# A fixed order for every engine in a window-attention and SoLU kernel: four engines' instruction order moved from the tile scheduler to a list made in the kernel

## The chip, the cores and the metric

The kernel runs on one NeuronCore of a Trainium2 chip. Five engines work beside each other, each on its own queue of instructions in order: TensorE (PE) multiplies matrices, VectorE (DVE) and ScalarE (ACT) work elementwise, GpSimd (POOL) does elementwise work too but only on SBUF here, and SyncE (SP) issues the DMA transfers. The metric is the device time of one execution in microseconds (us), the median of several.

## The reference

Attention over a sliding window of 64 positions, for 8 batches of 576 positions and 8 heads of 64, and then a layer of 512 to 1024 to 512 with a softmax-weighted activation and a normalization:

```python
def _attn_ref(q, k, v):
    scores = scale * np.matmul(q, k.transpose(0, 1, 3, 2))
    mask = (rel >= 0) & (rel < window)
    scores = np.where(mask, scores, -1000000000.0)
    scores = scores - np.max(scores, axis=-1, keepdims=True)
    attn = np.exp(scores)
    attn = attn / (np.sum(attn, axis=-1, keepdims=True) + 1e-09)
    return np.matmul(attn, v)

def _moe_ref(x, w_in, w_out, g_ln):
    h = x @ w_in
    e = np.exp(h - np.max(h, axis=-1, keepdims=True))
    solu = h * (e / (np.sum(e, axis=-1, keepdims=True) + 1e-09))
    mu = np.mean(solu, axis=-1, keepdims=True)
    var = np.mean((solu - mu) ** 2, axis=-1, keepdims=True)
    ln = (solu - mu) / np.sqrt(var + 1e-06) * g_ln
    return ln @ w_out
```

The weights come as float64 and q, k, v as float32.

## The kernel before

The 4608 positions are cut into 36 tiles of 128. What happens to tile t:

- `load` brings q, k and two halves of v by DMA.
- `attn_scores`: PE makes pS (8 heads, one buffer); DVE adds the mask and takes the maxima, eight instructions (L184); ACT takes eight exps (L188); DVE makes the reciprocals (L192, L193); POOL scales by them, eight instructions (L195). The result is sS.
- `attn_transpose`: PE transposes sS into pA, two times four heads; ACT and DVE copy one half each to PT (L206).
- `attn_values`: PE makes pX; ACT rounds it to xH (L224), and DVE makes the rest, xL (L225).
- `moe_in`: 24 matmuls of 128x512 (L237) in two halves of 12 make ph, the first layer in three products (high times high, high times low, low times high). The texts call this ph(t). There is one ph buffer.
- `moe_norm` reads ph: DVE's maximum (L248), ACT's exp (L249), DVE's product (L250); then small DVE steps, ACT's square (L255), more small steps (L256, L257, L259), POOL's power (L258) and the normalization in two halves (L262).
- `moe_transpose` (PE into pT, ACT's yH, DVE's yL) and `moe_out` (24 matmuls, L284, the second layer; the texts call them po(t)), then ACT's copy ot and a store.

The weights are float64 in HBM, and before use each is taken apart into a high and a low part on the chip. This goes in 16 blocks of 128x512, eight for each layer. A block is: a load of 0.5 MB (wi_raw or wo_raw, four buffers), ACT's Abs (L112), four DVE instructions (L113 to L116), for the second layer a product with g on POOL (L118), ACT's cast to the high part (L119) and POOL's difference, the low part (L120). Three work buffers (wi_t, wo_t) hold blocks in progress.

The loop runs 39 iterations. Iteration t does the first half of ph(t), the transposes of tile t+1, the second half of ph(t), the norm of t, then the transposes of the second layer for tile t-3, the values of t+1, the scores of t+3, and po(t-3). Ahead of the loop stand the loads of tiles 0 to 3, the eight blocks of the first layer, and scores, transposes and values of the first tiles. The second layer's eight blocks are written in iterations 0 and 1; they are first needed in iteration 3, at po(0).

PE keeps the order in which the kernel is written (`manual_schedule` names PE alone). The order of the other engines, and of SP's transfers, is chosen by the tile framework's scheduler, which runs a timeline of its own and takes an instruction earlier where it stands in `tc.high_priority(offset=URGENT)`: the copies out of PSUM, and L248 to L250.

Of the kernel before, what the change touches and what calls it, by code (L numbers as in the profile page):

```python
# [32 lines left out]
def tile_window_attention_solu_moe(
# [67 lines left out]
    live = {}  # L101

    def weight_block(src, wH, wL, g, name):

# [7 lines left out]
        nc.scalar.activation(tf, hi.bitcast(F32), AF.Abs)  # L112
        nc.vector.tensor_scalar(tf, tf, EXP_LO, EXP_HI, ALU.max, ALU.min)  # L113
        nc.vector.tensor_scalar(t, t, 0x07FFFFFF, 3, ALU.bitwise_and, ALU.logical_shift_left)  # L114
        nc.vector.scalar_tensor_tensor(t, hi, -0x40000000, t, ALU.bitwise_and, ALU.bitwise_or)  # L115
        nc.vector.scalar_tensor_tensor(t, lo, 29, t, ALU.logical_shift_right, ALU.bitwise_or)  # L116
# [2 lines left out]
        nc.scalar.copy(wH, tf)  # L119
        nc.gpsimd.tensor_sub(wL, tf, wH.bitcast(F32))  # L120

    def prep_in(c, h):
        hs = slice(h * 512, (h + 1) * 512)
        weight_block(
            w_in[c * P:(c + 1) * P, 2 * h * 512:2 * (h + 1) * 512],
            w_inH[:, c, hs], w_inL[:, c, hs], None, f"wi_{c}_{h}")

    def prep_out(f):
        weight_block(
            w_out[f * P:(f + 1) * P, :], w_outH[:, f], w_outL[:, f], g_sb[:, f:f + 1], f"wo_{f}")  # L130
# [4 lines left out]

    def load(t):
        first = first_of(t)
        o = t * P
# [20 lines left out]
        live["qk", t] = q, k
        live["v", t] = vv  # L160

    def attn_scores(t):
# [4 lines left out]
        for p in range(NPAIR):
            for half in range(2):
                for r in range(2):
                    rs = slice(r * D, (r + 1) * D)  # L170
# [5 lines left out]
                    nc.tensor.matmul(  # L176
                        pS[half * WIN:(half + 1) * WIN, r, p],
                        q[rs, p, half * WIN:(half + 1) * WIN], keys, start=True, stop=True)
        sS = sb.tile([P, H, P], F32, tag="sS", name=f"sS_{t}", bufs=3)
        nmx = st.tile([P, H], F32, tag="nmx", name=f"nmx_{t}")  # L180
        sm = st.tile([P, H], F32, tag="sm", name=f"sm_{t}")
        for h in range(H):

            nc.vector.tensor_tensor_reduce(  # L184
                sS[:, h], pS[:, h % 2, h // 2], masks[first], scale=-SCALE, scalar=BIG,
                op0=ALU.add, op1=ALU.min, accum_out=nmx[:, h:h + 1])
        for h in range(H):
            nc.scalar.activation(  # L188
                sS[:, h], sS[:, h], AF.Exp, bias=nmx[:, h:h + 1], scale=-1.0,
                accum_out=sm[:, h:h + 1])  # L190
        rec = st.tile([P, H], F32, tag="rec", name=f"rec_{t}")
        nc.vector.tensor_scalar_add(rec, sm, 1e-9)  # L192
        nc.vector.reciprocal(rec, rec)  # L193
        for h in range(H):
            nc.gpsimd.tensor_scalar(sS[:, h], sS[:, h], rec[:, h:h + 1], 0.0, ALU.mult, ALU.add)  # L195
# [161 lines left out]
```

## Time and profile before

| what | value |
|---|---|
| median of 3 runs | 615.12 us (615.04 to 616.85) |
| the profiled execution itself | 617.23 us |
| its span, first to last instruction | 615.4 us |
| mean granted TensorE clock | 0.972 |
| PE matmuls busy | 568.9 us, 92% |
| DVE, ACT, POOL busy | 316.3, 310.7, 217.7 us |

The span is what the profile's views cover; the time of an execution is 1.8 us more. A profile is of one execution. Every view names instructions by engine, by line of the kernel (L237 is line 237), and by tiles, output ahead of input, with buffer numbers left out. A wait is put down to what ended it. PE's busy time includes matmuls that only run slowly because the granted clock is low, so clock and busy time are read together.

### The profile page before, as it was taken

The numbers are of one execution on the slowest core, as the hardware profiler recorded it, in microseconds if no ns is written. First come the engines' busy times: TensorE is split into PE (matmuls) and PEld (weight loads), VectorE is DVE, ScalarE is ACT, GpSimd is POOL, SyncE is SP. The second block draws the span as 40 slices with busy tenths as digits, with TensorE's granted clock in tenths as the row PEclk, the third lists the DMA queues.
The fourth block names the chain that finished last, engine by engine and source line by source line (L and its number), as shares of the span: only waits on it lengthen the run. The fifth ranks groups of instructions, "written<-read, shape, count | busy, mean of one in ns | idle before, by whom it ended". The sixth has DMA issues, their size and how long they took to land.

```text
span 615.4 us, 12587 instructions
## 1 busy us (share of the span) xinstructions
PE 568.9 (92%) x4608; PEld 461.7 (75%) x4608; DVE 316.3 (51%) x1180; ACT 310.7 (50%) x933; POOL 217.7 (35%) x438
## 2 busy tenths in 40 slices
PE   1566589999999999999999999999999999999997
PEld 1334468888888888888888888888888888888775
DVE  2788955444444444444444455555454444443430
ACT  3555566555555555555555555555555555553331
POOL 2686864333333333333333333333333333331110
PEclk9966889999999999999999999999999999999999
DMA  8974422333333323333333333323333321000000
GB/s 280 322 227 158 134 78 79 96 99 98 98 98 98 96 94 96 95 95 95 95 96 95 95 95 96 95 95 95 95 95 95 95 95 53 18 18 18 18 35 34
DMA packets 56205, 60.97 MB, mean 99 GB/s; under 512 B 3408, under 2 KB 40272, under 8 KB 56144
## 3 DMA queue, kind: packets, MB, share of 16 engines
q1 hardware_dynamic: 56144, 60.18, 30.9%
q8 instruction: 36, 0.59, 0.4%
q14 instruction: 25, 0.20, 0.1%
HBM read 50.73 MB, written 9.44 MB: 98 GB/s over the span
## 4 chain that ended last, share of the span: by engine, by line
PE 86%; DVE 5%; POOL 3%; ACT 2%; DMA 1%; issue 1%; SPq 1%; POOLq 0%; ACTq 0%
PE po L284 34%; PE ph L237 31%; PE pX L218 6%; PE pS L176 5%; PE pA L204 5%; PE pT L273 5%; POOL sS L195 2%; DMA wi_raw<-w_in 1%; ACT sS L188 1%; DVE wo_t L113 1%; DVE wo_t L115 1%; POOL w_inL L120 1%; DVE e L250 1%; DVE wi_t L116 1%; DVE wo_t L114 0%
## 5 line engine op out<-in xcount | busy, mean ns | idle before, releaser
L237 PE MATMUL ph<-w_inH,xH 128*128 128x512 f32 x288 | 120.5, 419 | 14.1 <-DVE mst L250 6.1
L258 POOL TENSOR_TENSOR mst<-mst,neghalf 128x1 f32<-128x1 f32 x36 | 19.9, 554 | 317.2 <-DVE mst L257 317.2
L237 PE MATMUL ph<-w_inL,xH 128*128 128x512 f32 x288 | 117.6, 408 | 6.1 <-POOL w_inL L120 6.1
L284 PE MATMUL po<-w_outH,yH 128*128 128x512 f32 x288 | 117.7, 409 | 1.2 <-ACT yH L276 1.2
L237 PE MATMUL ph<-w_inH,xL 128*128 128x512 f32 x288 | 117.5, 408 | 0.5 <-DVE mst L252 0.5
L195 POOL TENSOR_SCALAR sS<-sS,rec 128x128 f32<-128x128 f32 x288 | 109.4, 401 | 18.0 <-ACT ot L287 10.0
L284 PE MATMUL po<-w_outH,yL 128*128 128x512 f32 x288 | 114.3, 397 | 0.0
L284 PE MATMUL po<-w_outL,yH 128*128 128x512 f32 x288 | 113.9, 395 | 0.0
L188 ACT ACTIVATE sS<-sS,nmx 128x128 f32<-128x128 f32 x288 | 111.2, 388 | 5.0 <-DVE nmx L184 5.0
L276 ACT CAST yH<-pT 128x512 fp32r<-128x512 f32 x72 | 38.7, 589 | 106.2 <-PE pT L273 106.2
L248 DVE TENSOR_REDUCE mst<-ph 128x1 f32<-128x1024 f32 x36 | 44.1, 1224 | 74.3 <-PE ph L237 74.3
L237 PEld LDWEIGHTS ph<-w_inH,xH 128*128 128x128 f32 x288 | 55.9, 194 | 27.1 <-DVE mst L250 6.4
L206 DVE COPY PT<-pA 128x512 f32<-128x512 f32 x36 | 24.9, 691 | 97.9 <-PE pA L204 97.9
L237 PEld LDWEIGHTS ph<-w_inL,xH 128*128 128x128 f32 x288 | 56.1, 195 | 19.9 <-POOL w_inL L120 8.3
L255 ACT ACTIVATE sq<-e,mst 128x1024 bf16<-128x1024 f32 x36 | 41.4, 1149 | 53.5 <-DVE mst L254 53.0
L284 PEld LDWEIGHTS po<-w_outH,yH 128*128 128x128 f32 x288 | 54.1, 188 | 18.5 <-ACT e L249 4.8
L237 PEld LDWEIGHTS ph<-w_inH,xL 128*128 128x128 f32 x288 | 56.1, 195 | 15.0 <-DVE mst L252 1.2
L284 PEld LDWEIGHTS po<-w_outH,yL 128*128 128x128 f32 x288 | 54.1, 188 | 14.6 <-DVE yL L277 1.7
L284 PEld LDWEIGHTS po<-w_outL,yH 128*128 128x128 f32 x288 | 54.2, 188 | 11.5
L262 POOL TENSOR_SCALAR e<-e,mst 128x512 f32<-128x512 f32 x72 | 55.8, 782 | 15.6 <-DVE mst L259 13.6
L206 ACT COPY PT<-pA 128x512 f32<-128x512 f32 x36 | 21.1, 586 | 78.8 <-PE pA L204 78.7
L188 ACT ACTIVATION_READ_ACCUMULATOR sS<-sS,nmx 128x1 f32 x288 | 53.8, 187 | 0.0
(59 smaller groups left out, 752.2 us busy)
## 6 DMA issues: line engine op xcount, KB each, us to landing
v<-vS SPq DMA_DIRECT2D x64, 256.0 KB, 2.9
k<-kT SPq DMA_DIRECT2D x35, 384.0 KB, 4.9
q<-qT SPq DMA_DIRECT2D x36, 256.0 KB, 4.1
y<-ot SPq DMA_DIRECT2D x36, 256.0 KB, 2.0
wi_raw<-w_in SPq DMA_DIRECT2D x8, 512.0 KB, 7.1
wo_raw<-w_out SPq DMA_DIRECT2D x8, 512.0 KB, 3.3
v<-vS SPq DMA_DIRECT2D x16, 128.0 KB, 2.9
k<-kT SPq DMA_DIRECT2D x1, 256.0 KB, 3.6
```

The costliest lines, as they stand in the source:

```text
L176: nc.tensor.matmul(pS[half * WIN:(half + 1) * WIN, r, p], q[rs, p, half * WIN:(half + 1) * WIN], keys, start=True, stop=True)
L188: nc.scalar.activation(sS[:, h], sS[:, h], AF.Exp, bias=nmx[:, h:h + 1], scale=-1.0, accum_out=sm[:, h:h + 1])
L195: nc.gpsimd.tensor_scalar(sS[:, h], sS[:, h], rec[:, h:h + 1], 0.0, ALU.mult, ALU.add)
L204: nc.tensor.transpose(pA[:, i], sS[:, 4 * x + i], ident)
L206: (nc.vector.tensor_copy if x else nc.scalar.copy)(PT[:, 4 * x:4 * x + 4], pA)
L218: nc.tensor.matmul(pX[r * D:(r + 1) * D, p, ks], vv[half][:, h * D:(h + 1) * D], PT[:, h, ks], start=True, stop=True)
L237: nc.tensor.matmul(live["h", t][:, hs], lhs[:, c], rhs[:, c, hs], start=(c == k == 0), stop=(c == NC - 1 and k == 2))
L248: nc.vector.tensor_reduce(nmax, ph, axis=AX.X, op=ALU.max, negate=True)
L255: nc.scalar.activation(sq, e, AF.Square, bias=nmean, scale=1.0, accum_out=ss)
L262: nc.gpsimd.tensor_scalar(e[:, hs], e[:, hs], nmean, kk, ALU.add, ALU.mult)
L276: nc.scalar.copy(yH[:, hs], pT)
L284: nc.tensor.matmul(po, lhs[:, f], rhs[:, f], start=(f == k == 0), stop=(f == NF - 1 and k == 2))
```

## The change

The kernel no longer leaves the order of DVE, ACT, POOL and SP to the framework. Each operation is first recorded, with its engine, a cost in ns, what it reads and writes, and a function that emits it. A ring says how many buffers a tile name has. `Plan.edges` makes dependencies from reads, writes and rings, and chains PE's operations in the order in which they are written. `Plan.order` gives each operation a due time (working back from a PE that never waits), then runs the list in time: whenever an engine is free, it takes of the operations that are ready the one that is due first. The instructions are then emitted in that order, and `manual_schedule` names all five engines. The high priorities are gone. The rings of nmx, sm and rec are 4 deep where they had 6 buffers; the others keep their depth. A score, a set of transposes and a set of values are each one operation of PE.

```diff
+RINGS = {
+    "raw": 4, "wt": 3, "q": 3, "k": 3, "v0": 4, "v1": 4, "sS": 3, "PT": 2, "xH": 2, "xL": 2,
+    "e": BEHIND + 1, "sq": 1, "yH": 1, "yL": 1, "ot": 2, "nmx": 4, "sm": 4, "rec": 4, "mst": 6,
+    "pS": 1, "pH": 1, "t": 2, "pX": 1, "pO": 1,
+}
+class Plan:
+    LATENCY = 150
...
+    def op(self, engine, cost, emit, reads, writes, lat=0):
+        self.ops.append((engine, cost, emit, reads, writes, lat + self.LATENCY))
+    def dma(self, size, emit, reads, writes):
+        self.op("SP", max(350, size // 250), emit, reads, writes, 2000)
...
+    def order(self):
...
+        clock, due = 0, [1e9] * n
+        for i, o in enumerate(self.ops):
+            if o[0] == "PE":
+                due[i] = clock
+                clock += o[1]
+        for j in reversed(topo):
+            for i, whole in after[j]:
+                lat = self.ops[j][5] if self.ops[i][0] != self.ops[j][0] else 0
+                due[j] = min(due[j], due[i] - (self.ops[j][1] + lat if whole else 0))
...
+        while any(waiting.values()):
+            begin, e = min(
+                (max(free[e], min(ready[i] for i in w)), e) for e, w in waiting.items() if w)
+            i = min((i for i in waiting[e] if ready[i] <= begin), key=lambda i: (due[i], i))
+            waiting[e].remove(i)
+            out.append(i)
+            end = begin + self.ops[i][1]
+            free[e] = end
...
-        nc.scalar.activation(tf, hi.bitcast(F32), AF.Abs)
-        nc.vector.tensor_scalar(tf, tf, EXP_LO, EXP_HI, ALU.max, ALU.min)
+        plan.op("ACT", 600, lambda: nc.scalar.activation(tf(), hi().bitcast(F32), AF.Abs), [R], [W])
+        plan.op("DVE", 420, lambda: nc.vector.tensor_scalar(
+            tf(), tf(), EXP_LO, EXP_HI, ALU.max, ALU.min), [W], [W])
...
-        with tc.high_priority(offset=URGENT):
-            nc.vector.tensor_reduce(nmax, ph, axis=AX.X, op=ALU.max, negate=True)
+        plan.op("DVE", 1150, lambda: nc.vector.tensor_reduce(
+            nmax(), PH(t), axis=AX.X, op=ALU.max, negate=True), [("pH", t)], [key(0)])
...
-    with tc.manual_schedule(engines={mybir.EngineType.PE}):
...
+    order = plan.order()
+    with tc.manual_schedule(engines={
+            mybir.EngineType.PE, mybir.EngineType.DVE, mybir.EngineType.Activation,
+            mybir.EngineType.Pool, mybir.EngineType.SP}):
+        for emit in order:
+            emit()
```

In what follows a row is an instruction as it stands on its engine: line, operation, output from input. The changed kernel's names are raw and wt for a weight block's load and work buffer (0 to 7 first layer, 8 to 15 second), t for the transposes' PSUM buffer, pH and pO for ph and po. Its lines: L257 to L263 are L113 to L116 of before, L266 is L118, L269 is L120, L353 is L184, L371 is L195, L392 is L206, L418 is L225, L449 and L454 are L248 and L250, L463 is L256.

SP at the program's start. Before:

```order
L142 DMA q_0_112<-qT 128x4x128
L146 DMA k_0_113<-kT 128x4x128
L155 DMA v0_0_116<-vS 64x512 x2
L157 DMA v1_0_119<-vS 128x512
L108 DMA wi_0_0_raw_121<-w_in 128x1024
L108 DMA wi_1_0_raw_131<-w_in 128x1024
L142 DMA q_1_188<-qT 128x4x128
```

Now:

```order
L255 DMA raw_0_112<-w_in 128x1024
L255 DMA raw_1_114<-w_in 128x1024
L255 DMA raw_2_116<-w_in 128x1024
L255 DMA raw_3_123<-w_in 128x1024
L303 DMA k_0_133<-kT 128x4x128
L300 DMA q_0_141<-qT 128x4x128
L255 DMA raw_4_148<-w_in 128x1024
```

Four weight loads have moved ahead of tile 0's q and k, and tile 0's v stands behind the fifth and sixth.

POOL from its first weight block on. Before:

```order
L120 TENSOR_TENSOR w_inL_104<-wi_0_0_t_123,w_inH_103 128x512
L195 TENSOR_SCALAR sS_0_158<-sS_0_158,rec_0_177 128x128 x8
L120 TENSOR_TENSOR w_inL_104<-wi_1_0_t_133,w_inH_103 128x512
L120 TENSOR_TENSOR w_inL_104<-wi_2_0_t_198,w_inH_103 128x512
L120 TENSOR_TENSOR w_inL_104<-wi_3_0_t_208,w_inH_103 128x512
L195 TENSOR_SCALAR sS_1_246<-sS_1_246,rec_1_265 128x128 x8
L120 TENSOR_TENSOR w_inL_104<-wi_0_1_t_307,w_inH_103 128x512
```

Now:

```order
L269 TENSOR_TENSOR w_inL_104<-wt_0_118,w_inH_103 128x512
L269 TENSOR_TENSOR w_inL_104<-wt_1_125,w_inH_103 128x512
L269 TENSOR_TENSOR w_inL_104<-wt_2_135,w_inH_103 128x512
L269 TENSOR_TENSOR w_inL_104<-wt_3_145,w_inH_103 128x512
L269 TENSOR_TENSOR w_inL_104<-wt_4_188,w_inH_103 128x512
L371 TENSOR_SCALAR sS_0_176<-sS_0_176,rec_0_211 128x128 x8
L269 TENSOR_TENSOR w_inL_104<-wt_5_213,w_inH_103 128x512
L269 TENSOR_TENSOR w_inL_104<-wt_6_242,w_inH_103 128x512
L371 TENSOR_SCALAR sS_1_271<-sS_1_271,rec_1_353 128x128 x8
```

Five first-layer blocks stand ahead of tile 0's scaling, where one stood; DVE's order at the start moved in the same way.

DVE around the first read of ph, tile 0's. Before:

```order
L116 SCALAR_TENSOR_TENSOR wo_1_t_414<-wo_1_raw_412,wo_1_t_414 128x512
L114 TENSOR_SCALAR wo_2_t_425<-wo_2_t_425 128x512
L248 TENSOR_REDUCE mst_0_492<-ph_0_454 128x1
L115 SCALAR_TENSOR_TENSOR wo_2_t_425<-wo_2_raw_423,wo_2_t_425 128x512
L113 TENSOR_SCALAR wo_3_t_436<-wo_3_t_436 128x512
L116 SCALAR_TENSOR_TENSOR wo_2_t_425<-wo_2_raw_423,wo_2_t_425 128x512
L114 TENSOR_SCALAR wo_3_t_436<-wo_3_t_436 128x512
L250 ISA e_0_493,mst_0_492<-ph_0_454,e_0_493 128x1024
```

Now:

```order
L392 COPY PT_1_401<-t_5_407 128x512
L366 TENSOR_SCALAR rec_2_422<-sm_2_377 128x8
L369 RECIPROCAL rec_2_422<-rec_2_422 128x8
L449 TENSOR_REDUCE mst_0_456<-pH_0_342 128x1
L418 TENSOR_TENSOR xL_1_484<-pX_1_438,xH_1_478 128x512
L353 ISA sS_3_486,nmx_3_487<-pS_3_460,maskNone_96 128x128
```

The second layer's blocks no longer stand around tile 0's two reads; between them are now xL and four of tile 3's scores (one is shown).

More of the change, by code (lines that the diff above doesn't have):

```diff
@@ L122, in prep_in, with T @@
[L122 to L130, printed above, removed]
+    plan = Plan(RINGS)
+    def T(tag, n, shape, dtype=F32, pool=None):
+        if (tag, n) not in plan.tiles:
+            plan.tiles[tag, n] = (pool or sb).tile(
+                shape, dtype, tag=tag, name=f"{tag}_{n}", bufs=RINGS[tag])
+        return plan.tiles[tag, n]
@@ new lines, in prep, with Q @@
+    def prep(i):
+        if i < 2 * NC:
+            h, c = divmod(i, NC)
+            hs = slice(h * 512, (h + 1) * 512)
+            weight_block(
+                i, w_in[c * P:(c + 1) * P, 2 * h * 512:2 * (h + 1) * 512],
+                w_inH[:, c, hs], w_inL[:, c, hs], None, ("in", c, h))
+        else:
+            f = i - 2 * NC
+            weight_block(
+                i, w_out[f * P:(f + 1) * P, :], w_outH[:, f], w_outL[:, f], g_sb[:, f:f + 1],
+                ("out", f))
+    def Q(t):
+        return T("q", t, [P, NPAIR, P])
@@ L136, in load, with K, V @@
+    def K(t):
+        return T("k", t, [P, NPAIR, P + WIN])
+    def V(t, half):
+        return T(f"v{half}", t, [P, DM])
     def load(t):
@@ new lines, in softmax @@
+        plan.op("DVE", 130, lambda: nc.vector.tensor_scalar_add(
+            rec(), T("sm", t, [P, H], pool=st), 1e-9),
+            [("sm", t, h) for h in range(H)], [("rec", t)])
+        plan.op("DVE", 130, lambda: nc.vector.reciprocal(rec(), rec()), [], [("rec", t)])
+        for h in range(H):
+            plan.op("POOL", 360, lambda h=h: nc.gpsimd.tensor_scalar(
+                SS(t)[:, h], SS(t)[:, h], rec()[:, h:h + 1], 0.0, ALU.mult, ALU.add),
+                [("rec", t)], [("sS", t, h)])
@@ L279, in moe_out, with PO @@
+            plan.op("DVE", 620, lambda hs=hs, pT=pT: nc.vector.tensor_sub(
+                YL(t)[:, hs], pT(), YH(t)[:, hs].bitcast(F32)),
+                [("t", n), ("yH", t, h)], [("yL", t, h)])
     def moe_out(t):
[L280 to L281 removed]
+        def PO():
+            return T("pO", t, [P, DM], pool=ps_o)
         for f in range(NF):
[L283 to L285 removed]
@@ L286, in moe_out @@
-        ot = sb.tile([P, DM], F32, tag="ot", name=f"ot_{t}")
-        nc.scalar.copy(ot, po)
-        nc.sync.dma_start(out[t * P:(t + 1) * P, :], ot)
+            for k, (y, w, keys) in enumerate((
+                    (YH, w_outH, ["yH", "H"]), (YH, w_outL, ["yH", "L"]), (YL, w_outH, ["yL", "H"]))):
+                plan.op("PE", 233, lambda f=f, k=k, y=y, w=w: nc.tensor.matmul(
+                    PO(), y(t)[:, f], w[:, f], start=(f == k == 0), stop=(f == NF - 1 and k == 2)),
+                    [(keys[0], t, f // 4), (keys[1], "out", f)], [("pO", t)])
```

418 lines of the change are left out of this document (262 added, 156 removed).

## The prediction

> **What bounds the kernel now.** First the page: how full TensorE (PE) is, and where.
>
> ```profile
> span 615.4 us, 12587 instructions
> PE   1566589999999999999999999999999999999997
> PEclk9966889999999999999999999999999999999999
> ```
>
> The rows are forty slices of 15.4 us: PE's busy tenths and its granted clock. From the seventh slice on PE is full and its clock is whole, so an order can win only in front of that. The table by stage says how much there is:
>
> ```profile
> 20.00:40.00 20.00, 13.87 (x125) 9.38 (x125) 15.86 (x55) 11.88 (x43) 13.20 (x18) 0.90 0.93 301
> 40.00:60.00 20.00, 10.44 (x77) 6.54 (x78) 16.89 (x29) 9.22 (x16) 15.76 (x17) 0.59 0.48 161
> 60.00:80.00 20.00, 13.02 (x102) 10.32 (x101) 18.11 (x62) 11.49 (x37) 16.80 (x20) 0.76 0.34 107
> 100.00:150.00 50.00, 50.00 (x413) 41.08 (x404) 26.88 (x117) 26.72 (x83) 14.81 (x34) 1.00 0.35 110
> ```
>
> After the length stand PE, its weight loads, DVE, ACT, POOL, clock, DMA. Between 20 and 80 us DVE and POOL are the full ones; PE idles and runs below its clock. The chain of waits shows where the regular part begins:
>
> ```profile
> 100.25 5.79 PE po L284 x24
> 115.50 5.79 PE po L284 x24
> ```
>
> From the first output matmul, po(0), at 100.25 every tile takes 115.50 - 100.25 = 15.25 us of gapless PE; 515.1 us remain to the span's end. PE's instructions and their order stay the same. So the end moves by what po(0) moves, plus any new wait behind it. Next PE's waits before 110 us (who was waited for, us, times, longest), and PE's starts after them:
>
> ```profile
> PE pA L204 <- POOL sS L195: 13.8, 5, 11.5
> PE ph L237 <- DVE mst L250: 6.1, 1, 6.1
> PE ph L237 <- POOL w_inL L120: 6.1, 3, 4.2
> PE ph L237 <- ACT w_outH L119: 4.0, 1, 4.0
> ...
> 4.96 1.99 PE L176 MATMUL pS<-k,q 64*64 64x128 f32 x32 [4.96 <-DMA k<-kT]
> 30.73 0.50 PE L237 MATMUL ph<-w_inH,xH 128*128 128x512 f32 x1 [1.92 <-ACT xH L224]
> 50.27 1.02 PE L218 MATMUL pX<-PT,v 128*64 128x64 f32 x14
> 57.59 0.77 PE L237 MATMUL ph<-w_inH,xH 128*128 128x512 f32 x1 [3.97 <-ACT w_outH L119]
> 76.50 0.79 PE L237 MATMUL ph<-w_inH,xH 128*128 128x512 f32 x1 [6.11 <-DVE mst L250]
> 88.84 0.47 PE L237 MATMUL ph<-w_inH,xH 128*128 128x512 f32 x1 [1.80 <-DVE mst L253]
> ```
>
> So ph(0), the first-layer matmuls of tile 0, starts at 30.73 and ends by 50.27; ph(1) to ph(3) start at 57.59, 76.50, 88.84. Before each of the last three PE waits until DVE and ACT have read the one ph buffer (L248 maximum, L249 exp, L250 product). What DVE does in the longest of these waits:
>
> ```profile
> 71.07 1.21 DVE L248 TENSOR_REDUCE mst<-ph 128x1 f32<-128x1024 f32 x1
> 73.00 0.60 DVE L113 TENSOR_SCALAR wo_t<-wo_t 128x512 f32<-128x512 f32 x1 [0.72 <-ACT wo_t L112]
> 73.64 0.48 DVE L114 TENSOR_SCALAR wo_t<-wo_t 128x512 int32<-128x512 int32 x1
> 74.04 0.67 DVE L225 TENSOR_TENSOR xL<-pX,xH 128x512 fp32r<-128x512 f32 x1
> 74.63 0.68 DVE L115 SCALAR_TENSOR_TENSOR wo_t<-wo_raw,wo_t 128x512 int32<-128x512 int32 x1
> 75.23 1.21 DVE L250 CUSTOM_DVE_ANT_0 e<-ph,e 128x1024 f32<-128x1024 f32 x1
> ```
>
> PE stands still for these rows, and steps of the second layer's weights (wo), which nothing needs before po(0), run among them. One more limit lies underneath:
>
> ```profile
> 13.90 0.68 DVE L116 SCALAR_TENSOR_TENSOR wi_t<-wi_raw,wi_t 128x512 int32<-128x512 int32 x1
> 14.50 0.42 DVE L114 TENSOR_SCALAR wi_t<-wi_t 128x512 int32<-128x512 int32 x1
> 16.30 1.64 DVE L116 SCALAR_TENSOR_TENSOR wi_t<-wi_raw,wi_t 128x512 int32<-128x512 int32 x1
> 16.12 1.27 POOL L120 TENSOR_TENSOR w_inL<-wi_t,w_inH 128x512 fp32r<-128x512 f32 x1 [11.47 <-ACT w_inH L119]
> 17.37 5.52 POOL L195 TENSOR_SCALAR sS<-sS,rec 128x128 f32<-128x128 f32 x8
> 305.31 2.82 POOL L195 TENSOR_SCALAR sS<-sS,rec 128x128 f32<-128x128 f32 x8 [0.43 <-ACT ot L287]
> ```
>
> L116 takes 0.68 alone and 1.64 beside POOL's L120, of which 1.09 is L120's rest; POOL's eight L195 take 2.82 alone and 5.52 beside weight work. DVE's weight instructions and POOL's work exclude each other. A weight block thus costs 2 x 0.42 + 2 x 0.68 = 2.2 us of DVE, 2.3 with the steps between, plus 1.27 of POOL: about 3.3 when blocks follow each other.
>
> **The change part by part.** No arithmetic instruction is added or removed, and PE's order is as it was. The orders of DVE, ACT, POOL and SP become a fixed list, which I follow to po(0).
>
> *Start to ph(0).* Four weight blocks go ahead of tile 0's scores on SP, DVE and POOL. The first block (0.5 MB) should land at about 5.0, as the first 0.5 MB (q and k) did before PE's start at 4.96. The loads queued behind the four on SP (k, q, then v, which waits behind the fifth block's free buffer) land well before pS(0) and pX(0) can use them. ACT 0.66, DVE 2.3: 8.0; three more blocks at 3.3: 17.9 to 18.4. Eight scores at 0.21 (L184's starts): 20. Eight exps follow:
>
> ```profile
> L188 ACT ACTIVATE sS<-sS,nmx 128x128 f32<-128x128 f32 x48 | 18.6, 388 | 5.0 <-DVE nmx L184 5.0
> ```
>
> 8 x 0.388 + an Abs of 0.66: 23; the reciprocal 0.4; POOL is in the fifth block's L120 until 24.5, then L195, between 2.82 and 5.52, say 4.0: 28.5. Last transposes 0.7, pS(1) 2.0 and pX(0) 2.0 at half clock, xH 0.6: **ph(0) at 33.9, 3.2 later** (bounds 1 to 6: L195's two prices, and the landing up to 2 us off).
>
> *ph(0).* Its first half needs weight blocks 0 to 3, done by now: 12 x 0.233 = 2.8. The second half waits for tile 1's transposes, behind exp, and for blocks 4 to 7. DVE from 20 on: four blocks 9.2, scores, a copy, xL and reciprocals 3.9, and 3.5 of waiting behind POOL (three L120): 36.6. Then POOL: tile 1's L195, from 37.5 to 41.5, and the last L120 until 42.7, just ahead of its use. Second half from 41.7 at half clock, 12 x 0.427 = 5.1: ends 46.8. So 12.8 us in place of 50.27 - 30.73 = 19.5: **-6.7** (-3 to -9).
>
> *After ph(0).* L248 1.2, exp 1.1 + 0.2, four scores 0.85, L250 1.2: 4.6 in place of 57.59 - 50.27 = 7.3, with no wo step between: **-2.7** (-3.3 to 0). ph(1) at 51.4.
>
> *ph(1) to ph(2).* Before 76.50 - 57.59 = 18.9. Now the first half takes between 3 and 5.1 by the clock, I take 4.2; transposes 0.8 and second half 3.05: 8.1. Then L248 1.2, exp 1.3, four scores 0.85, xL 0.7, L250 1.2: 5.3, together 13.4. **-5.5** (-7 to -2). ph(2) at 64.8.
>
> *ph(2) to ph(3).* Before 12.3. The wo blocks that were put off now come here: 5.1 at half clock + 0.8 + 3.05, then the same reads with one more score and 0.8 of wo, less xL, 5.6: 14.6. **+2.3** (0 to +4). ph(3) at 79.4.
>
> *ph(3) to po(0).* 11.4 before; the same PE work, its first half again partly at half clock: 11.3, **-0.1** (-1 to +1). **po(0) at 90.7, 9.5 earlier.**
>
> *po(0) itself.* The last rows of second-layer weights:
>
> ```profile
> L120 POOL TENSOR_TENSOR w_outL<-wo_t,w_outH x8: 1272/1312/1748, 50.6 to 81.5; 128x512 fp32r<-128x512 f32 x8
> ```
>
> Before, POOL ends them at 81.5 + 1.3, 17 us ahead of po(0). Now DVE has, from 42.7 on, eight blocks 18.4, three tiles' scores 5.1, four tiles' reads 9.8, seven copies and differences of 0.69, and 1.5 of small ones: 39.6. POOL's share of these blocks and three tiles' L195 are 25, of which I let half stand in DVE's way: 94.8, and L118, ACT's cast and L120 of the last block are half hidden: about 96.8. po(0) wants the eighth block at 90.7 + 22 x 0.233 = 95.8: **+1** (0 to +6, if none or nearly all of the 25 stands in the way).
>
> Sum: +3.2 - 6.7 - 2.7 - 5.5 + 2.3 - 0.1 + 1 = **-8.5**. The profiled execution took 617.2, 615.4 of span and 1.8 around it, and would take 608.7. The median of the three runs shown is 615.12, 2.1 below it; I take the same loss off that: **606.6**.
>
> *Without effect:* SP's later loads (landing 3 to 5 us, wanted a period later); rings of 4 in place of 6 for nmx, sm, rec, since tile t+3 is the furthest ahead; the tail, where ACT's order is as before. Each would cost its wait once if that cover went.
>
> *The clock.* What a partly idle PE does to its clock:
>
> ```profile
> 87.10:90.50 3.40, 1.66 (x7) 1.21 (x8) 3.04 (x17) 1.71 (x8) 1.50 (x2) 0.99 0.87 266
> 90.50:93.90 3.40, 3.40 (x12) 2.72 (x11) 1.04 (x10) 3.40 (x14) 0.55 (x1) 0.50 0.24 80
> ```
>
> After 3.40 us in which PE was busy 1.66 the clock was 0.50. So I count on half clock behind gaps of 2 to 3 us. [...]
>
> **The rivals.**
> *Clock stays whole.* The gaps before ph(1) to ph(3) are now 4.6 to 5.6, of which pX and pS fill about 2.2, so PE never idles longer than 2.4 to 3.4. If that doesn't lower the clock, ph(0)'s second half and the first halves of ph(1) to ph(3) save up to 2.3, 1.1, 2.3, 1.6, of which some returns as waits: -5, **601.5**. Against it stand the rows above. 0.12. [...]
>
> *Weights too late.* DVE and POOL are the true bound: both orders must do 16 blocks of 3.3 and eight g products of 0.7, 58 us, before po(0) ends. If the put-off wo blocks end 4 to 6 us later than 96.8, po(0) waits: **611**. For it: both engines over 75% busy from 20 to 80. 0.13.
>
> *Slower: a wait in every tile.* In the regular part DVE's scale product (L256, now L463) stands ahead of the copy of PT, and waits for ACT's square, which now comes after the eight exps.
>
> ```profile
> 304.59 0.56 ACT L287 COPY ot<-po 128x512 f32<-128x512 f32 x1
> 308.05 0.69 DVE L206 COPY PT<-pA 128x512 f32<-128x512 f32 x1 [2.90 <-PE pA L204]
> ```
>
> The exps and the square together still end at 304.6, and PE's transposes let the copy start at 308.05: 3 us of slack, with two small instructions taken off. Lateness beyond that is paid by all 33 regular tiles; from 0.26 us beyond (8.5/33) the kernel is slower, at 0.6 it takes **626**. Nothing in the rows takes up the slack. 0.05.
>
> *Nothing gained.* The start costs its bound, +6, ph(0) gains only 3 and ph(1) only 2: 606.6 + 2.8 + 3.7 + 3.5 = **616.6**. 0.06.
>
> **How the numbers follow.** The forecast, 604 to 610, has 0.64, the rivals what stands at them. The range 601.5 to 611.5 takes in the clock and most of the late weights; it leaves out the two dear cases and the edges of the first two, about 0.18. A run tells 0.3%, 1.8 us, from no change: faster 0.89, same 0.06, slower 0.05.
>
> **What would show it.** ph(0) near 34 (later than before), ph(1) near 51, ph(2) 65, ph(3) 79, po(0) 91; from po(1) on a period of 15.25; no wo row between L449 and L454 of tile 0; the last w_outL after po(0)'s start; half clock in ph(2). Wrong if ph(0) starts after 37, if po(0) waits over 2 us for w_outL, or if the period grows.

## The result and the profile after

The changed kernel takes **604.58 us** (median of 4 runs, 604.1 to 605.04) against 615.23 us of the kernel before (4 runs, 615.04 to 616.85): a ratio of 0.982, 95% interval 0.980 to 0.984. The profiled execution took 604.69 us, 602.5 of it span. These are the rows of the page that answer to those of before (forty slices, now of 15.1 us: PE's busy tenths, its granted clock):

```profile
span 602.5 us, 12551 instructions
PE   1387699999999999999999999999999999999997
PEclk9988889999999999999999999999999999999999
```

PE is full from the sixth slice on, one slice earlier, and the clock falls in four slices as before, to 8 in place of 6 and 8. By stage (length, PE, weight loads, DVE, ACT, POOL, clock, DMA):

```profile
40.00:60.00 20.00, 17.00 (x173) 13.35 (x172) 13.96 (x41) 11.71 (x36) 10.33 (x20) 0.83 0.40 138
60.00:80.00 20.00, 14.36 (x108) 11.34 (x109) 18.48 (x61) 13.34 (x44) 13.78 (x18) 0.85 0.80 240
```

Most of PE's gain is in 40 to 60 us: 17.0 us busy at clock 0.83, where it was 10.4 at 0.59. DVE is less busy there than before (13.96 us for 16.89) and fuller afterwards (18.48 for 18.11): work was put off. PE's starts after its waits, and then the chain of waits behind them:

```profile
32.80 0.50 PE L434 MATMUL pH<-w_inH,xH 128*128 128x512 f32 x1
...
48.95 0.50 PE L434 MATMUL pH<-w_inH,xH 128*128 128x512 f32 x1 [2.36 <-DVE mst L454]
62.27 0.50 PE L434 MATMUL pH<-w_inH,xH 128*128 128x512 f32 x1 [2.92 <-DVE mst L454]
76.08 0.47 PE L434 MATMUL pH<-w_inH,xH 128*128 128x512 f32 x1 [3.37 <-DVE mst L454]
```

```profile
44.47 1.10 PE pX L411 x32
...
87.41 5.80 PE pO L508 x24
102.69 5.79 PE pO L508 x24
117.94 5.79 PE pO L508 x24
```

ph(0) to ph(3) start at 32.80, 48.95, 62.27 and 76.08, po(0) at 87.41, and behind it a tile takes 15.28 and then 15.25 us as before. The waits after ph(0) to ph(2) are 2.4, 2.9 and 3.4 us where those of before were 4.0, 6.1 and 1.8. The end moved by 615.4 - 602.5 = 12.9, po(0) by 100.25 - 87.41 = 12.8: nothing changed behind po(0). What DVE does in the first of these waits (tile 0):

```profile
44.51 1.23 DVE L449 TENSOR_REDUCE mst<-pH 128x1 f32<-128x1024 f32 x1 [2.81 <-PE pH L434]
46.22 0.69 DVE L418 TENSOR_TENSOR xL<-pX,xH 128x512 fp32r<-128x512 f32 x1 [0.48 <-ACT xH L417]
46.83 0.28 DVE L353 CUSTOM_DVE_ANT_0 sS<-pS,maskNone 128x128 f32<-128x128 f32 x1
...
47.66 1.22 DVE L454 CUSTOM_DVE_ANT_0 e<-pH,e 128x1024 f32<-128x1024 f32 x1
```

No second-layer step stands there; four scores and xL do. And the put-off blocks' last step, on POOL (first and last start at the row's end):

```profile
L269 POOL TENSOR_TENSOR w_outL<-wt,w_outH x8: 1272/1304/1810, 57.6 to 91.1; 128x512 fp32r<-128x512 f32 x8
```

It starts at 91.1 and ends near 92.4. po(0) wants it at its 23rd matmul, 87.34 + 22 x 0.233 = 92.5. Nothing is left over: that matmul's weight load waited 0.2 us for it.

### The profile page after: what moved, and what is told of

Same layout as the page of the kernel before. It is cut to its first block, busy times and chain, and to the rows that moved or that the text cites. A ratio compares the mean times of both kernels' runs of the same rounds, so it can differ in the third digit from the quotient of the medians.

```text
span 602.5 us, 12551 instructions
## 1 busy us (share of the span) xinstructions
PE 563.9 (94%) x4608; PEld 459.3 (76%) x4608; DVE 322.0 (53%) x1180; ACT 313.3 (52%) x933; POOL 210.2 (35%) x438
## 4 chain that ended last, share of the span: by engine, by line
PE 90%; DVE 5%; ACT 2%; POOL 1%; DMA 1%; issue 1%; SPq 0%; ACTq 0%
PE pO L508 35%; PE pH L434 34%; PE pX L411 6%; PE t L387 6%; PE pS L340 5%; PE t L491 5%; DVE wt L261 1%; DMA raw<-w_in 1%; DVE wt L263 1%; DVE sS L353 1%; DVE e L454 1%; POOL sS L371 1%; ACT sS L358 1%; POOL w_inL L269 0%; DVE wt L259 0%
## 5 line engine op out<-in xcount | busy, mean ns | idle before, releaser
L371 POOL TENSOR_SCALAR sS<-sS,rec 128x128 f32<-128x128 f32 x288 | 105.0, 386 | 258.6 <-PE pO L508 257.1
L434 PE MATMUL pH<-w_inH,xH 128*128 128x512 f32 x288 | 119.2, 414 | 8.6 <-DVE mst L454 8.6
L508 PE MATMUL pO<-w_outH,yH 128*128 128x512 f32 x288 | 117.7, 409 | 1.2 <-ACT yH L495 1.2
L434 PE MATMUL pH<-w_inH,xL 128*128 128x512 f32 x288 | 116.3, 404 | 0.0
L434 PE MATMUL pH<-w_inL,xH 128*128 128x512 f32 x288 | 116.0, 403 | 0.0
L508 PE MATMUL pO<-w_outH,yL 128*128 128x512 f32 x288 | 114.3, 397 | 0.0
L508 PE MATMUL pO<-w_outL,yH 128*128 128x512 f32 x288 | 113.9, 395 | 0.0
L449 DVE TENSOR_REDUCE mst<-pH 128x1 f32<-128x1024 f32 x36 | 44.1, 1224 | 70.5 <-PE pH L434 70.5
L392 DVE COPY PT<-t 128x512 f32<-128x512 f32 x36 | 24.9, 691 | 89.5 <-PE t L387 89.5
L434 PEld LDWEIGHTS pH<-w_inH,xH 128*128 128x128 f32 x288 | 55.3, 192 | 21.0 <-DVE mst L454 5.8
L508 PEld LDWEIGHTS pO<-w_outH,yH 128*128 128x128 f32 x288 | 54.1, 188 | 18.5 <-ACT e L451 4.8
L434 PEld LDWEIGHTS pH<-w_inH,xL 128*128 128x128 f32 x288 | 55.4, 192 | 13.5 <-DVE xL L418 0.2
L508 PEld LDWEIGHTS pO<-w_outH,yL 128*128 128x128 f32 x288 | 54.1, 188 | 14.6 <-DVE yL L497 1.7
L434 PEld LDWEIGHTS pH<-w_inL,xH 128*128 128x128 f32 x288 | 55.5, 193 | 11.7
L508 PEld LDWEIGHTS pO<-w_outL,yH 128*128 128x128 f32 x288 | 54.2, 188 | 11.6 <-POOL w_outL L269 0.2
L392 ACT COPY PT<-t 128x512 f32<-128x512 f32 x36 | 21.1, 585 | 76.5 <-PE t L387 76.5
L353 DVE CUSTOM_DVE_ANT_0 sS<-pS,maskNone 128x128 f32<-128x128 f32 x224 | 51.3, 286 | 14.0 <-PE pS L340 14.0
L387 PE MATMUL t<-ident,sS 128*128 128x128 f32 x288 | 42.0, 283 | 12.9 <-POOL sS L371 12.7
```

The lines of the kernel that those rows point to most:

```text
L353: plan.op("DVE", 215, lambda h=h: nc.vector.tensor_tensor_reduce(SS(t)[:, h], PS(t)[:, h % 2, h // 2], mk, scale=-SCALE, scalar=BIG, op0=A ...
L371: plan.op("POOL", 360, lambda h=h: nc.gpsimd.tensor_scalar(SS(t)[:, h], SS(t)[:, h], rec()[:, h:h + 1], 0.0, ALU.mult, ALU.add), [("rec", ...
L387: nc.tensor.transpose(pA()[:, i], SS(t)[:, 4 * x + i], ident)
L392: (nc.vector.tensor_copy if x else nc.scalar.copy)(PT(t)[:, 4 * x:4 * x + 4], pA()),
L434: plan.op("PE", 233, lambda c=c, k=k, x=x, w=w: nc.tensor.matmul(PH(t)[:, hs], x(t)[:, c], w[:, c, hs], start=(c == k == 0), stop=(c == NC ...
L449: plan.op("DVE", 1150, lambda: nc.vector.tensor_reduce(nmax(), PH(t), axis=AX.X, op=ALU.max, negate=True), [("pH", t)], [key(0)])
```

## The experiments

All kernels' milestones together (starts of ph(0) to ph(3), po(0) and po(1) in one profiled execution each, us) with the timed medians. Each ratio is to the runs of the kernel before that were made beside it.

| kernel | ph(0) | ph(1) | ph(2) | ph(3) | po(0) | po(1) | median | ratio, 95% |
|---|---|---|---|---|---|---|---|---|
| before | 30.7 | 57.6 | 76.5 | 88.8 | 100.2 | 115.4 | 615.23 | 1 |
| changed | 32.8 | 49.0 | 62.3 | 76.1 | 87.3 | 102.6 | 604.58 | 0.980 to 0.984 |
| e1 second layer early | 33.0 | 54.1 | 66.2 | 89.4 | 99.4 | 114.6 | 616.64 | 1.000 to 1.003 |
| e6 reads give way | 33.5 | 52.4 | 73.7 | 90.5 | 101.8 | 117.1 | 618.62 | 1.004 to 1.007 |
| e2 low parts on DVE | 28.8 | 46.8 | 59.9 | 71.9 | 83.0 | 99.7 | 602.38 | 0.975 to 0.981 |
| e3 gaps filled | 32.9 | 47.8 | 59.6 | 73.1 | 82.8 | 100.3 | 602.47 | 0.976 to 0.980 |
| e4 list for PE, DVE | 35.2 | 52.5 | 66.7 | 81.9 | 93.0 | 108.3 | 608.20 | 0.985 to 0.990 |
| e7 list for all but DVE | 34.5 | 47.4 | 59.0 | 74.8 | 87.2 | 102.9 | 605.43 | 0.982 to 0.986 |
| e8 scores first | 33.9 | 48.6 | 61.4 | 74.6 | 85.8 | 101.1 | 603.02 | 0.978 to 0.981 |
| e5 before again | 29.2 | 56.1 | 75.0 | 87.5 | 97.3 | 112.5 | 614.29, one | |
| e9 = e2 + e3 | 29.7 | 45.7 | 58.7 | 70.8 | 80.4 | 97.4 | 599.09 | 0.971 to 0.975 |
| e10 = e9, g on ACT | 30.0 | 46.1 | 58.6 | 70.6 | 80.2 | 96.8 | 599.65 | 0.971 to 0.974 |
| e11 = e9 + e8 | 32.6 | 46.7 | 60.0 | 72.1 | 81.7 | 98.2 | 600.21 | 0.973 to 0.976 |

### e1 and e6: the second layer's steps among the reads again

The planner gets a number that is added to an operation's due time. In e1 it makes the second layer's blocks 30 us more urgent, in e6 it makes the read L454 of tiles 0 to 2 less urgent by 20 us.

```diff
+        self.early[len(self.ops)] = self.bias
...
+        due = [d + self.early[i] for i, d in enumerate(due)]
...
+    plan.bias = -30000
     for i in range(8, 16):
         prep(i)
+    plan.bias = 0
```

> The changed kernel, with the second layer's eight blocks given a due time 30 us earlier, so that their steps are taken as soon as they are ready and stand among the reads of ph again. Theory (putting the second layer's steps behind the reads is what took the waits away): ph(0) still starts at 32 to 36, but the waits for L454 after ph(0) to ph(2) grow from 2.4, 2.9 and 3.4 us to 5 or more each and the clock falls for longer: po(0) at 97 to 104, the kernel at 613 to 619. Rival (the gain is that of the start and of ph(0) alone, and the reads are not what counts): po(0) at 87 to 90, 604 to 607.

e1 lost the whole gain, as the theory said, but at another place. PE's waits before 115 us (lines stand 3 later here):

```profile
PE pS L343 <- DMA q<-qT: 15.6, 2, 11.8
...
PE pX L414 <- DVE PT L395: 11.3, 1, 11.3
```

The reads of tiles 0 and 1 were not touched. Between 67.4 and 85.7 us DVE went through the steps of the last five second-layer blocks, eight of them between tile 2's two reads, and the copy of PT stood behind them all: PE waited 11.3 us for that copy, and would otherwise have waited for the second read, which came right behind it. A further 3.8 us went into a wait for q, since the edit makes the second layer's loads more urgent too. So e1 shows that early second-layer steps cost the gain, not that they cost it between the reads. e6 was made for that:

```diff
+        plan.bias = 20000 if t < 3 else 0
         plan.op("DVE", 1150, lambda: nc.vector.tensor_tensor_reduce(
             E(t), PH(t), E(t), scale=1.0, scalar=0.0, op0=ALU.mult, op1=ALU.add, accum_out=sp()),
...
+        plan.bias = 0
```

> The changed kernel, in which DVE's product (L454) of tiles 0 to 2 alone has a due time 20 us later, so that four more scores and the four steps of a second-layer block stand between L449 and L454 of tile 0, and the like in tiles 1 and 2. The loads' order and the start are as in the changed kernel. Theory (second-layer steps among the reads cost PE's waits what they take): the wait behind ph(0) grows from 2.4 us by 0.85 + 2.2 to 5 or more, those behind ph(1) and ph(2) alike, with more half clock: po(0) at 97 to 103, the kernel at 613 to 619. Rival (what cost the time in the run with early second-layer blocks was only DVE standing still for loads that had not landed): po(0) at 88 to 92, 605 to 609.

DVE in tile 0 of e6 (L449 is L452 here, L454 is L458), and PE's waits:

```profile
44.79 1.23 DVE L452 TENSOR_REDUCE mst<-pH 128x1 f32<-128x1024 f32 x1 [2.75 <-PE pH L437]
...
48.79 0.42 DVE L260 TENSOR_SCALAR wt<-wt 128x512 f32<-128x512 f32 x1
49.25 0.43 DVE L262 TENSOR_SCALAR wt<-wt 128x512 int32<-128x512 int32 x1
49.71 0.69 DVE L264 SCALAR_TENSOR_TENSOR wt<-raw,wt 128x512 int32<-128x512 int32 x1
50.44 0.69 DVE L266 SCALAR_TENSOR_TENSOR wt<-raw,wt 128x512 int32<-128x512 int32 x1
51.05 1.22 DVE L458 CUSTOM_DVE_ANT_0 e<-pH,e 128x1024 f32<-128x1024 f32 x1
```

```profile
PE pH L437 <- DVE mst L458: 17.0, 2, 10.5
...
PE pH L437 <- DVE rec L369: 5.5, 1, 5.5
```

The four steps take 2.3 us between the two reads, and the wait behind ph(0) is 5.5 in place of 2.4 us. The next two are 10.5 and 6.5. (The first is put down to rec, L369, which started as L458 ended; what the matmul waits for is L458.) Between tile 1's reads stood ten weight steps (in the changed kernel two), between tile 2's four (there one), and in each tile three or four more scores. The three waits grew from 8.6 to 22.5 us in all, by 13.9, and the kernel lost 14.0 against the changed one. The eleven more scores make 11 x 0.21 = 2.3 us of that, an estimate from their spacing; the rest falls to the weight steps and what they wait for. The theory holds, and at its place.

### e2: the low parts on DVE

```diff
-        plan.op("POOL", 1300, lambda: nc.gpsimd.tensor_sub(wL, tf(), wH.bitcast(F32)),
+        plan.op("DVE", 690, lambda: nc.vector.tensor_sub(wL, tf(), wH.bitcast(F32)),
                 [W, ("H", *key)], [("L", *key)])
```

> The changed kernel, with the low part of all 16 weight blocks (L269) computed by DVE in place of POOL. Theory (DVE's weight steps and POOL's work exclude each other, so that a block costs the sum of both): a block falls from 2.2 + 1.27 = 3.5 us of the two engines together to 2.2 + 0.69 = 2.9, although DVE gets 16 x 0.69 = 11 us more to do; no L261 of 1.7 us is left in the first 20 us, ph(0) starts at 29 to 31 and po(0) at 82 to 85.5: 599 to 603. Rival (DVE alone is the full engine and POOL has room): the 11 us come on top where DVE is busy 14 to 18.5 of 20 us, po(0) at 89 to 94: 606 to 611.

The same line in the first 20 us of the changed kernel, and then of e2 (busy us, mean ns):

```profile
L261 DVE SCALAR_TENSOR_TENSOR wt<-raw,wt 128x512 int32<-128x512 int32 x5 | 6.5, 1298 | 0.2
```

```profile
L261 DVE SCALAR_TENSOR_TENSOR wt<-raw,wt 128x512 int32<-128x512 int32 x5 | 3.5, 699 | 0.1
```

With POOL's L269 gone L261 falls from 1.30 to 0.70 us, ph(0) comes 4 us earlier and po(0) 4.3, although DVE has 11 us more to do: exclusion is a limit underneath, and DVE's own time isn't the only one. A part of the 4 us has another cause: in the changed kernel POOL is in the fifth block's L269 (22.13 to 23.39) when tile 0's reciprocals are ready at 21.92, and starts its scaling 1.5 us later; in e2 it starts 0.2 us after them. Exclusion holds the other way too. POOL's scaling, now beside DVE's weight steps, takes longer than the 4.0 and 3.3 us of the changed kernel for tiles 0 and 1:

```profile
18.05 5.30 POOL L371 TENSOR_SCALAR sS<-sS,rec 128x128 f32<-128x128 f32 x8 [13.41 <-ACT wt L256]
32.10 5.51 POOL L371 TENSOR_SCALAR sS<-sS,rec 128x128 f32<-128x128 f32 x8 [8.75 <-DVE rec L369]
```

Of the 4.3 us at po(0) 2.9 are left at po(1): inside po(0) PE waits for the last blocks.

### e3: PE's gaps filled

```diff
+    def keep_warm(t, n):
+        def emit():
+            po = T("pO", 0, [P, DM], pool=ps_o)
+            for _ in range(n):
+                nc.tensor.matmul(po, XH(t)[:, 0], w_inH[:, 0, :512], start=True, stop=True)
+        if n:
+            plan.op("PE", 0, emit, [("xH", t), ("H", "in", 0, 0)], [("pO", 0)])
...
         on(moe_in, t, 0)
+        if t == 0:
+            keep_warm(0, 6)
...
         on(softmax, t + AHEAD)
+        if t < 3:
+            keep_warm(t, (8, 10, 12)[t])
```

> The changed kernel, with matmuls whose result is thrown away put into PE's gaps: 6 behind the first half of ph(0), and 8, 10 and 12 ahead of ph(1), ph(2) and ph(3), each of the 128x512 form, written to the buffer of po(0), which the first real matmul there overwrites. Theory (the partly idle stretches lower the clock, and that costs): the four runs of twelve matmuls that took 4.28, 4.51, 4.24 and 4.45 us take 2.8 each, po(0) comes 2 to 6 us earlier (it stays behind the last w_outL for some of it): 599 to 602.5. Rival 1 (the weight blocks on DVE and POOL set po(0) whatever PE does, as the last w_outL landed just when po(0) wanted it): the matmuls are faster and the waits longer by as much: 603.5 to 605.5. Rival 2 (the clock falls for another reason): the runs of twelve stay above 4 us, and the time at 604 to 606.

First the changed kernel in stretches of 3.413 us whose edges are those at which its clock changes (PE's busy time and count come first, the clock is the third number from the end):

```profile
36.42:39.84 3.42, 2.35 (x8) 1.02 (x9) 2.31 (x17) 2.77 (x13) 3.42 (x10) 1.00 1.00 365
39.84:43.25 3.41, 3.41 (x9) 2.76 (x10) 1.06 (x3) 1.42 (x7) 2.52 (x5) 0.51 1.09 361
...
46.66:50.08 3.42, 1.13 (x5) 0.96 (x6) 3.42 (x20) 3.42 (x13) 0.00 (x0) 1.00 0.00 0
50.08:53.49 3.41, 3.41 (x11) 2.56 (x10) 2.64 (x7) 1.40 (x8) 1.13 (x2) 0.51 0.09 17
...
60.31:63.73 3.42, 1.46 (x6) 1.24 (x7) 3.42 (x20) 3.42 (x16) 1.27 (x1) 1.00 0.98 249
63.73:67.14 3.41, 3.41 (x11) 2.68 (x10) 2.72 (x7) 1.06 (x5) 1.98 (x4) 0.51 0.29 82
...
70.55:73.97 3.42, 2.16 (x65) 1.85 (x64) 3.38 (x9) 2.26 (x5) 2.50 (x4) 1.00 0.88 287
73.97:77.38 3.41, 1.30 (x5) 0.97 (x6) 3.41 (x13) 3.24 (x14) 3.41 (x5) 1.00 1.04 328
77.38:80.79 3.41, 3.41 (x11) 2.61 (x10) 3.34 (x12) 1.94 (x6) 1.21 (x1) 0.51 0.88 273
```

Four whole stretches run at half clock, each behind one in which PE worked only partly (for the first, see the last section). They are ph(0)'s second half and the first halves of ph(1) to ph(3). In e3 no stretch is left at half clock (mean clock 0.999 in place of 0.989). The twelve matmuls of ph(2)'s first half, in the chain of the changed kernel and of e3:

```profile
62.27 4.24 PE pH L434 x12
```

```profile
59.61 3.07 PE pH L434 x12
```

po(0) starts 4.6 us earlier, so half clock costs that much there. But inside po(0), e3 waits for DVE:

```profile
84.78 0.50 PE L508 MATMUL pO<-w_outH,yL 128*128 128x512 f32 x1 [1.30 <-DVE yL L497]
...
90.19 0.50 PE L508 MATMUL pO<-w_outL,yH 128*128 128x512 f32 x1 [0.48 <-DVE mst L463]
```

(The second row reads w_outL, whose last L269 started at 88.8.) At po(1) 2.3 of the 4.6 us are left, in the timed runs 2.1. The theory and rival 1 are each half right: the clock has that price, and DVE's work and the weight blocks take half of it back.

### e4 and e7: which engine's order

```diff
-    with tc.manual_schedule(engines={
-            mybir.EngineType.PE, mybir.EngineType.DVE, mybir.EngineType.Activation,
-            mybir.EngineType.Pool, mybir.EngineType.SP}):
+    with tc.manual_schedule(engines={mybir.EngineType.PE, mybir.EngineType.DVE}):
```

> The changed kernel, with the fixed list for PE and DVE alone; ACT, POOL and SP are left to the framework, which starts from the list's order. Theory (DVE's order makes the gain: the reads of ph free of the second layer's steps): 604 to 607, po(0) at 87 to 90. Rival (the order of the others carries a good part, since POOL's work holds DVE up and ACT's casts come ahead of POOL's): ph(0) starts at 36 or later, 610 to 614.

608.20 lies between the two: with the list for DVE and PE alone 7.7 us are left of the gain (615.94, the runs of before beside it, less 608.20). In the profile, of its slowest execution (609.98), ph(0) starts 2.4 us later, and the waits for L454 grow from 8.6 us in all:

```profile
PE pH L434 <- DVE mst L454: 11.8, 3, 5.4
```

In e7 the set holds all but DVE.

> The changed kernel, with the fixed list for PE, ACT, POOL and SP; DVE alone is left to the framework, which starts from the list's order and keeps the second layer's steps behind L454 of tile 0, with one or two of them among the reads of tiles 1 and 2. Theory (it is not DVE's exact row order that counts, but that the steps come late, and that POOL's and ACT's weight work stands in the list's order): po(0) at 86 to 90, 603 to 607. Rival (DVE's exact order carries the gain): 609 to 614.

605.43: with DVE left to the framework nearly the whole gain stays. DVE's exact row order is not what counts. In both kernels the framework starts from the list, so that the second layer's steps come late (in e7 none stands between tile 0's reads, three between tile 1's, two between tile 2's); and POOL's, ACT's and SP's order carries about 3 us of the gain (10.65 - 7.7). It shows in the end of ph(0): 48.0 in e4 and 43.2 in e7, where the changed kernel has 44.4 and the kernel before 50.3.

### e5: the kernel before once more

> The kernel before, once more, for a second profile of it. The first profiled execution took 617.2 us, 2.0 more than the median of its runs, and the traces of before and of the changed kernel stand 12.9 us apart where the timed runs stand 10.65 apart. Theory (the first profiled execution lost time of its own in the stretch before po(0), where waits and half clock meet differently from one execution to the next): an execution near 615 shows po(0) at 98 to 99 and the same 15.25 us per tile behind it. Rival (the 2 us lie in the regular part or around the span): po(0) again at 100 to 100.5.

This execution took 614.29 us, and po(0) starts at 97.3, 2.9 earlier than in the first, with the same 15.25 behind it. Half of the difference lies ahead of ph(0) (29.2 against 30.7), the other half in ph(3), which here runs at whole clock behind the same gap of 1.80 us. What differs is how the gap lies to the edges at which the clock changes. First this execution, whose clock rises at 79.11, in stretches of 3.413 us from there, then the first execution with its edges:

```profile
85.93:89.35 3.42, 1.86 (x8) 1.36 (x9) 3.23 (x19) 1.73 (x9) 1.31 (x2) 1.00 0.81 252
89.35:92.76 3.41, 3.41 (x20) 2.88 (x19) 1.74 (x11) 3.41 (x15) 0.81 (x2) 1.00 0.25 84
```

```profile
87.05:90.46 3.41, 1.62 (x7) 1.17 (x8) 3.00 (x17) 1.72 (x8) 1.52 (x2) 1.00 0.85 261
90.46:93.87 3.41, 3.41 (x12) 2.73 (x11) 1.08 (x10) 3.41 (x15) 0.55 (x1) 0.50 0.26 84
```

Behind 1.86 us of work in a stretch the clock stayed whole, behind 1.62 it fell. So the kernel before varies in itself: beside e1 to e4 its 13 executions took 614.4 to 618.3. The four of the changed kernel lie within 1 us.

### e8: tile 0's scores first

```diff
+    plan.bias = -40000
     load(0)
+    plan.bias = 0
...
+    plan.bias = -40000
     scores(0)
     softmax(0)
+    plan.bias = 0
```

> The changed kernel, with the loads and the scores of tile 0 ahead of the weight blocks on SP, PE, DVE, ACT and POOL, as in the kernel before. Theory (DVE's and POOL's work up to the end of ph(0) sets the time, not when ph(0) starts): ph(0) starts 2 to 6 us earlier, at 27 to 31, but ends no earlier than in the changed kernel (44.4) as the weight blocks come later by what DVE and POOL wait for tile 0's exps: 604 to 609. Rival (the later start of ph(0) is 2 us of loss): the time falls by those 2 us or more, to 600 to 603.

Both missed, the theory by 1 us and in the start of ph(0), the rival in that ph(0) never started earlier. The first transposes come at 11.9 in place of 24.0, yet ph(0) starts at 33.9: PE's order puts pX(0) and the next scores ahead of it. These now wait 4.1 us for tile 1's q, and then 3.5 us for the copy of PT and 3.5 for DVE's scores (nmx), which stand behind weight steps.

ph(0) ends at 44.1 (44.4 in the changed kernel), which agrees with the thought that DVE's and POOL's work sets that end. Between ph(1) and ph(3) 1.2 us are gained, since the waits for L454 are shorter; why is left open. The two ratios' intervals touch, so that the 1.6 us between the medians are not certain.

### e9 to e11: both edits together

> The changed kernel with both edits: the low parts on DVE and the matmuls that fill PE's gaps. Theory (each took away a wait of its own, 2.2 and 2.1 us): 599.5 to 601. Rival (both run into the same bound, DVE's last second-layer block, which ended at 89.5 and 90.1 in the two runs): po(0) starts at 79 to 82 and then waits 2 us or more for w_outL, 601.3 to 602.7.

599.09, 5.5 below the changed kernel, where the two edits alone add up to 4.3. Whether that is more than their sum is open: at po(1) the traces have 2.9 and 2.3 for the edits alone and 5.2 for both, and the timed runs of e9 were made beside other runs of the kernel before than those of e2 and e3. The rival's shared bound, at any rate, did not take the second gain away. PE still stops for the last block inside po(0), and DVE is the full engine (e9, 60 to 80 us):

```profile
87.23 0.50 PE L508 MATMUL pO<-w_outL,yH 128*128 128x512 f32 x1 [0.68 <-DVE w_outL L269]
```

```profile
60.00:80.00 20.00, 19.77 (x200) 16.08 (x202) 19.25 (x50) 13.67 (x41) 7.59 (x12) 1.00 0.68 212
```

Next, the product with g goes from POOL to ACT:

```diff
-            plan.op("POOL", 700, lambda: nc.gpsimd.tensor_scalar(
-                tf(), tf(), g, 0.0, ALU.mult, ALU.add), [W, ("g",)], [W])
+            plan.op("ACT", 600, lambda: nc.scalar.activation(
+                tf(), tf(), AF.Copy, scale=g), [W, ("g",)], [W])
```

> As the run with both edits, and the product of the second layer's blocks with g (L266) computed by ACT in place of POOL. Theory (POOL's eight products of 0.7 to 1.1 us hold DVE up, and ACT has room): the last block ends 2 to 4 us earlier than in the run with both edits, and the kernel gains what po(0) waited there, 598 to 600. Rival (ACT becomes the engine that is waited for, with 13 to 14 of 20 us busy, or DVE's own time is all that counts): within 0.7 us of the run with both edits, or slower.

599.65, no difference: the last block started at 85.9 in place of 86.5. So it isn't POOL's products that hold it now. DVE is 19.5 of 20 us busy between 60 and 80; that its own work is the last limit was not tried.

> The run with both edits (low parts on DVE, PE's gaps filled), and tile 0's loads and scores ahead of the weight blocks. Theory (the 1.6 us that the scores' place brought alone come on top): 597 to 598.6. Rival (with both edits DVE has no idle time left to give, 18 to 19 of 20 us busy from 40 on, and starting its blocks 6 us later puts the last one off): the last w_outL later than 86.5, 599 to 602.

600.21: the scores' place doesn't add up with the rest. The last w_outL starts at 87.3, later than in e9, as the rival has it. **e9 has the lowest median of all that were run**, 0.973 (0.971 to 0.975) of the kernel before; the intervals of e10 and e11 overlap with it.

## Why the prediction was right, and what it mis-sized

The forecast was 606.6 in a range of 601.5 to 611.5, and 604.58 came. By its own terms, in us of the profiled executions:

| term | predicted | measured | how |
|---|---|---|---|
| start to ph(0) | +3.2 | +2.1 | 32.80 for 30.73 |
| ph(0) | -6.7 | -7.9 | 44.40 - 32.80 = 11.6 for 19.5 |
| gap after ph(0) | -2.7 | -2.8 | 48.95 - 44.40 = 4.6 for 7.3 |
| ph(1) to ph(2) | -5.5 | -5.6 | 13.32 for 18.91 |
| ph(2) to ph(3) | +2.3 | +1.5 | 13.81 for 12.34 |
| ph(3) to po(0) | -0.1 | -0.1 | 11.33 for 11.41 |
| inside po(0) | +1 | 0 | 15.28 for 15.25 |
| sum | -8.5 | -12.8 | |

The measured column is against the first execution of the kernel before. Against the second (e5) the start is +3.6, ph(3) to po(0) +1.5, and po(0) moves by 9.9 in all. The milestones themselves don't hang on that: 33.9, 51.4, 64.8, 79.4 and 90.7 were forecast for ph(0) to ph(3) and po(0), and 32.8, 49.0, 62.3, 76.1 and 87.4 came. The other signs came too: no wo row between L449 and L454 of tile 0, the last w_outL behind the start of po(0), half clock in ph(2).

- **Up to po(0) every term had the right sign**, and the two that rest on the reads (the gap after ph(0), and ph(1) to ph(2)) were right to 0.1 us. e6 shows their cause.
- **Start.** Mis-sized by 1.1. The first block was counted at 5.0 plus ACT's 0.66; DVE's first weight step began at 4.71, not 5.7, and up to L371 the rest followed as counted (3.3 us a block, L371 4.00). Behind L371 the sum came out by luck. It had pX(0) at half clock, 2.0 us, and it took 1.15; and it had left out pS(2), which PE's order puts ahead of ph(0) and which cannot start until DVE has read pS(1), at 31.66. PE's scores of tiles 1 and 2, the first 1.97 us long for 1.10, though the clock column reads 1.00 there:

```profile
27.84 1.97 PE L340 MATMUL pS<-k,q 64*64 64x128 f32 x32
...
31.76 1.10 PE L340 MATMUL pS<-k,q 64*64 64x128 f32 x32 [0.87 <-PE pX L411]
```

- **ph(0).** Mis-sized by 1.2. The second half began 7.1 us behind the start of ph(0), not 7.8, since tile 1's L371 took 3.27 in place of 4; and it took 4.5, not 5.1, since the clock was whole again from 43.25 on. A large part of this largest term shows on POOL: the kernel before scaled a later tile ahead of a first-layer block that PE waited for, and now the last block comes first. Before:

```profile
41.59 4.64 POOL L195 TENSOR_SCALAR sS<-sS,rec 128x128 f32<-128x128 f32 x7
...
47.51 0.79 PE L237 MATMUL ph<-w_inL,xH 128*128 128x512 f32 x1 [4.20 <-POOL w_inL L120]
```

Now:

```profile
39.70 1.28 POOL L269 TENSOR_TENSOR w_inL<-wt,w_inH 128x512 fp32r<-128x512 f32 x1
41.87 2.83 POOL L371 TENSOR_SCALAR sS<-sS,rec 128x128 f32<-128x128 f32 x8 [0.90 <-DVE rec L369]
```

- **ph(2) to ph(3).** Mis-sized by 0.8: its first half took 4.0 us, not 5.1, since half clock began only at 63.73, and the transposes 1.2 for 0.8.
- **The put-off blocks.** The sum had the last w_outL end at 96.8; it ended at 92.4. The 4.4 us divide so. The first layer was done at 40.98, not 42.7. From there DVE's last weight step ended after 47.3 us, at 88.26, where the sum had 52.1 (39.6 of DVE's own work and 12.5 for half of POOL's 25):

```profile
40.98:88.26 47.28, 38.64 (x375) 30.83 (x374) 39.36 (x111) 29.59 (x85) 27.03 (x41) 0.87 0.51 160
```

DVE was busy for 39.4 us of that. Its weight steps (L257 to L263) took 21.5 of them, where eight blocks alone are 8 x 2.24 = 17.9, so that about 3.6 us of standing in the way are left in place of 12.5; 7.9 us DVE was idle, which the sum did not have. The last block then took 4.2 us in place of 2.0. The wait of +1 wasn't there, but no room was left either: as soon as PE came earlier (e2, e3, e9) it appeared.
- **The step that was wrong in kind** is the last one, from the profiled execution to the median. The sum made 608.7 for an execution, and 2.1 were taken off, the distance by which the profiled execution of before lay above its median. But that was a property of that one execution (e5: 2.9 us between two of them, all ahead of po(0)), and the changed kernel's profiled execution stands at its median. 606.6 was as close as it is by luck: the two errors, 4.0 too high and 2.1 too low, partly cancel.
- **The clock.** Half clock came where it was counted, in ph(0)'s second half and the first halves of ph(1) to ph(3). The rival in which it stays whole fell; e3 gives the price, 4.6 us at po(0), of which 2.1 to 2.3 reach the end.
- **Weights too late** did not come, with nothing to spare. **A wait in every tile** did not come: the period is 15.25, and in the middle of the program the copy of PT still waits for PE's transposes, with this much room:

```profile
310.48 0.69 DVE L392 COPY PT<-t 128x512 f32<-128x512 f32 x1 [2.76 <-PE t L387]
```

- **What the change owes its gain to.** Of the 12.8 us at po(0), 5.8 are won by the end of ph(0), and 8.4 in the two terms of the reads, of which ph(2) to ph(3) gives 1.5 back. e4's theory had argued the gain as DVE's order. e7 corrects that: what counts for the reads is that second-layer steps come late in the sequence from which all engines are ordered; DVE's rows may be chosen by the framework. The 5.8 us no run takes alone; e4, where ph(0) ends at 48.0, speaks for POOL's, ACT's and SP's order. Not tried was the kernel before with its second-layer blocks merely written later and the order left to the framework, so it stays open how much of the gain needs a fixed list at all.
